# Convolution and soft mixture of experts on one core: the tap softmax in token layout, its result sent through a DRAM buffer into the diagonals of zeroed band tiles

## The chip, the cores and the metric

The kernel runs on one core of a Trainium2 chip. Such a core has a matrix engine (PE, with its weight loads shown apart as PEld), a vector engine (DVE), a scalar engine (ACT), a general engine (POOL), and an engine that only issues transfers (SP, its queue is SPq in the profile). Each engine works through its own list of instructions in order; they meet only at semaphores. Transfers between DRAM and on-chip memory (SBUF) run on 16 DMA engines. The metric is the device time of one execution in microseconds (us); lower is better.

## The reference, cut to what matters

Two layers in a row: a convolution over 7 tokens whose weights are a softmax made per token and head, and a soft mixture of experts over all 28672 tokens.

```python
# attention-like convolution: B, S, D = 8, 3584, 192; H, K = 8, 7 (24 channels a head)
w = exp(weight_gen - max(weight_gen, -1));  w = w / (sum(w, -1) + 1e-09)      # per token and head
x_pad = concatenate([zeros(B, 6, D), x], 1);  x_unf = x_pad[:, s + k]           # 7 rows a token
out = einsum('bshk,bskhg->bshg', w, x_unf)                                      # (B, S, 192)
# soft mixture: N = 28672 tokens, 8 experts with 4 slots each, F = 1024
logits = x @ phi                                                                # (N, 32)
d = softmax over tokens of logits;  slot_input = d.T @ x                        # (32, 192)
slot_out[e] = relu(slot_input[e] @ w1[e]) @ w2[e]
y = (softmax over slots of logits) @ slot_out
```

Everything is float32.

## The kernel before

**Tiling.** The 3584 tokens of a batch are cut into 35 groups of 104 tokens, a group into 4 blocks of 26 (`T`). So there are 280 groups. A block is convolved by one matmul per half of the heads: the stationary operand is a band matrix of 128 rows (4 heads with 32 input rows each) by 26 tokens, whose entry at row j + k, token j is the weight of tap k. The moving operand holds the input rows of the same 4 heads on the diagonal of a tile whose other parts are zero (`xbd`, in `big`), so that each head meets its own weights only. One call of `conv(p)` (L228) does a pair of groups, 16 matmuls, each recorded as two passes; there are 140 pairs, p = 0 to 139.

**Band tiles.** Seven groups make a superstep s (`SGG`, 40 of them). For each, `loadw` (L176) brings two copies of the taps: one in token rows, from which only the maximum is taken, and one already laid out by the host in band rows. `tap_top` (L181, DVE) takes the maximum of the 7 taps; `tap_spread` (L187, POOL) multiplies it by a mask; `tap_rows` (L194, PE) is a matmul with the constant `near`, which carries the maxima to the band rows (`pmx`); `tap_sub` (L199, DVE) and `tap_exp` (L203, ACT) follow; `band_make` (L206, POOL) multiplies the result by `mask2` into the full band tile. There are three band tiles and four taps tiles.

**Normalisation.** The softmax is not divided before the convolution. Each head has a 25th column of ones in `xbd` (`GX` = 25), so each matmul also gives the sum of the exponentials. `conv_sum` (L243, ACT) takes it out, `conv_inv` (L251, DVE) inverts it for two pairs at once, and `conv_out` (L255, DVE) multiplies it in while it copies the pair out of PSUM into `tm`.

**The rest of the main loop.** `xpose` (L264) turns the pair on PE and `xpose_out` copies it out; after each unit of 8 pairs (`UNITS`) come `logits` (L294), a running maximum, and `dispatch` (L356), which adds the unit to the slot inputs. Two pairs make a slot k of the loop at L523. After the main loop come the experts (L723 to L822) and the output phase (L834 to L846), which only multiplies, copies out and stores 22 MB.

**What sets the order.** All the engines' lists are written in one order: a planner (`op` and `model`, L480 to L693) is given for each step its engine, a cost, what it reads and writes, and for transfers a delay to landing; the order on PE and SP is the order in which the steps are listed, the other engines are chosen by due time. The opening (L376 to L436) is written out by hand. SP issues all transfers and is strictly in order, so a transfer that waits for a buffer holds up all those behind it. Transfers also share eight rotating semaphores, so a transfer cannot be issued before the one eight issues earlier has landed.

Of the kernel before, what the change touches and what calls it, by code (L numbers as in the profile page):

```python
# [8 lines left out]
F32 = mybir.dt.float32  # L9
# [7 lines left out]
GX = GW + 1  # L17
# [8 lines left out]
TAPS = NBC * KT  # L26
# [3 lines left out]
WARM = 9, 5  # L30
# [11 lines left out]
def conv_soft_moe(ctx, tc, xh, wh, phi, w1a, w1b, w2, out):  # L42
# [15 lines left out]
    NXH, HBC = 5, NBC // 2  # L58
    XB = 4 * HBC * GX
    big = keep.tile([128, NXH * XB], F32, name="big")  # L60
# [43 lines left out]
    NTM, NCV, NTAP, NBAND = 2, 3, 4, 3  # L104
    xbd = big.rearrange("p (i h c) -> p i h c", i=NXH, h=4)
    HB = NBC // 2


    taps = [fix.tile([128, 2, TAPS], F32, name=f"taps{i}") for i in range(NTAP)]
    bands = [fix.tile([128, T, NBC], F32, name=f"band{i}") for i in range(NBAND)]  # L110
# [5 lines left out]

    pmx = ps_l.tile([128, 512], F32, name="pmx")
    topP = pmx[:, 0:TAPS].rearrange("p (q l) -> p q l", q=KT)
# [13 lines left out]
    def warm(k):  # L132
        to = ps_t.tile([128, 4, 128], F32, tag="pt", name=f"warm{k}")[:, 0]
        for _ in range(WARM[k]):
# [3 lines left out]
    V.memset(one, 1.0)  # L138
    V.memset(xbd[:, 0:2, 0], 0.0)
    G.memset(xbd[:, 0:2, 1], 0.0)  # L140
    V.memset(xbd[:, 0:2, 2], 0.0)
    A.copy(xbd[:, 0:2, 3], zero.unsqueeze(1).to_broadcast([128, 2, HBC * GX]))
    ident = keep.tile([128, 128], F32, name="ident")
    make_identity(nc, ident)
    near = keep.tile([128, 128], F32, name="near")
    G.memset(near, 1.0)
    G.affine_select(out=near, in_=near, compare_op=ALU.is_ge, fill=0.0, base=0,
                    pattern=[[1, 128]], channel_multiplier=-1)
    G.affine_select(out=near, in_=near, compare_op=ALU.is_ge, fill=0.0, base=KT - 1,
                    pattern=[[-1, 128]], channel_multiplier=1)  # L150
    mask = keep.tile([128, 1, 32], F32, name="mask")
    maskT = keep.tile([128, 1, 32], F32, name="maskT")
    mask2 = keep.tile([128, 32, 1], F32, name="mask2")
    own = keep.tile([128, KT, 1], F32, name="own")

# [7 lines left out]
    eps = keep.tile([128, 1], F32, name="eps")  # L163
    V.memset(eps, EPS)
    for t in cvs:

        A.copy(t[:, 0 : 16 * GX], one.to_broadcast([128, 16 * GX]))

    def loadx(j):

        s, part = divmod(j, 2)
        z = slice(part * HBC * GX, (part + 1) * HBC * GX)
        for h in range(4):
            SY.dma_start(xbd[32 * h : 32 * h + 32, j % NXH, h], xh[s, h, :, z])  # L174

    def loadw(s):  # L176
        SY.dma_start(taps[s % NTAP], wh[s])

    tops = {}

    def tap_top(s):  # L181

        tops[s] = pa.tile([128, NBC, 1], F32, tag="top", name=f"top{s}")
        V.tensor_reduce(out=tops[s][:, :, 0], op=ALU.max, axis=AX.X,  # L184
                        in_=taps[s % NTAP][:, 0].rearrange("p (l k) -> p l k", k=KT))

    def tap_spread(s, eng=G):  # L187

        tops[s] = pa.tile([128, KT, NBC], F32, tag="spread", name=f"spread{s}"), tops[s]
        eng.tensor_tensor(out=tops[s][0], in0=own.to_broadcast([128, KT, NBC]),  # L190
                          in1=tops[s][1].rearrange("p l o -> p o l").to_broadcast([128, KT, NBC]),
                          op=ALU.mult)

    def tap_rows(s):  # L194

        P.matmul(pmx[:, 0:TAPS], near, tops[s][0].rearrange("p q l -> p (q l)"),  # L196
                 start=True, stop=True)

    def tap_sub(s):  # L199
        r = taps[s % NTAP][:, 1]  # L200
        V.tensor_tensor(out=r, in0=r, in1=pmx[:, 0:TAPS], op=ALU.subtract)  # L201

    def tap_exp(s):  # L203
        A.activation(taps[s % NTAP][:, 1], taps[s % NTAP][:, 1], AF.Exp)  # L204

    def band_make(s, lo=0, hi=HB, eng=G):  # L206

        l = slice(2 * lo, 2 * hi)
        r = taps[s % NTAP][:, 1].rearrange("p (q l) -> p q l", q=KT)[:, :, l]
        w = bands[s % NBAND]  # L210
        for j, n in ((0, 3 * KT), (3 * KT, T - 3 * KT)):
            k = min(n, KT)
            eng.tensor_tensor(out=w[:, j : j + n, l].rearrange("p (a k) l -> p a k l", k=k),  # L213
                              in0=r[:, 0:k].unsqueeze(1).to_broadcast([128, n // k, k, 2 * (hi - lo)]),
                              in1=mask2[:, j : j + n].rearrange("p (a k) o -> p a k o", k=k)
                              .to_broadcast([128, n // k, k, 2 * (hi - lo)]), op=ALU.mult)
# [11 lines left out]
    def conv(p):  # L228
        cv = cvs[p % NCV]
        for par in range(2):  # L230
            s, g = divmod(2 * p + par, SGG)
            for c in range(2):
                for blk in range(4):
                    bc = (4 * g + blk) * 2 + c
                    o = 4 * GX * (2 * par + (c ^ par))
                    j, b = divmod(s * NBC + bc, HBC)
                    P.matmul(cv[32 * blk : 32 * blk + T, o : o + 4 * GX],  # L237
                             bands[s % NBAND][:, :, bc],
                             xbd[:, j % NXH, :, b * GX : (b + 1) * GX], start=True, stop=True)

    wss = {}

    def conv_sum(p):  # L243

# [706 lines left out]
```

## Time and profile before

| | us |
|---|---|
| median of 3 runs | 344.33 |
| lowest and highest | 342.26, 345.93 |
| span of the profiled execution | 345.3 |
| DVE, ACT, POOL busy in it | 249.9, 161.7, 198.8 |
| first convolution matmul begins | 8.56 |
| first matmul of the output phase begins | 282.44 |

The page gives no other time of the profiled execution than its span, which lies 1.0 us above the median of the runs. Three stretches are told apart below: the opening until the loop runs evenly, the main loop until the last convolution, and what follows (experts and output). In the rows quoted, the first number of a piece in the chain of waits or of the timeline is its start in us, the second its length; in the groups of instructions it is busy us and mean ns of one, then the idle time of the engine ahead of them.

### The profile page before, as it was taken

Reading aid. Unit: us, or ns where it says so; the run is one execution under the profiler, and the core shown is the slowest. Engines: PE = TensorE matmul, PEld = TensorE weight load, DVE = VectorE, ACT = ScalarE, POOL = GpSimd, SP = SyncE. Lnnn points to the kernel's source line nnn. Section 1 sums busy time; section 2 is a strip of 40 time slices with the busy share of each in tenths; the row PEclk is TensorE's granted clock in tenths of the full one; section 3 lists DMA queues with packets and bytes.
Section 4 is the critical chain, followed back from the end, with each engine's and each line's share of the span. In section 5 each row is a group of like instructions: output and inputs, shape, how many; then the busy total and the mean of one; then the engine's idle time right before and its main releaser. Section 6 shows DMA issues by size and latency. Waiting matters only on the chain.

```text
span 345.3 us, 16352 instructions
## 1 busy us (share of the span) xinstructions
PE 306.8 (89%) x6896; PEld 222.2 (64%) x6896; DVE 249.9 (72%) x550; ACT 161.7 (47%) x428; POOL 198.8 (58%) x261
## 2 busy tenths in 40 slices
PE   8789999899999998999999999899997988799600
PEld 6567777687778876778778777678784952124100
DVE  7766877878788886897887868777864759965400
ACT  6535454455645654456445544454632237534300
POOL 8679648679489785868778568586601720000000
PEclk9999999999999999999999999999999999975555
DMA  6787788877877777677876867966589009999995
GB/s 197 215 260 196 214 223 196 246 205 221 215 217 228 211 235 189 199 207 205 241 210 176 237 173 204 260 172 180 154 307 364 6 2 398 395 403 399 395 404 204
DMA packets 33001, 80.82 MB, mean 234 GB/s; under 512 B 7072, under 2 KB 7456, under 8 KB 32928
## 3 DMA queue, kind: packets, MB, share of 16 engines
q1 hardware_dynamic: 32928, 79.77, 74.7%
q8 instruction: 55, 0.90, 1.2%
q14 instruction: 18, 0.15, 0.2%
HBM read 57.38 MB, written 22.36 MB: 231 GB/s over the span
## 4 chain that ended last, share of the span: by engine, by line
PE 58%; DMA 19%; DVE 9%; ACT 4%; issue 3%; SPq 2%; POOL 1%; DVEq 0%; ACTq 0%; POOLq 0%
PE cv L237 25%; PE pt L272 12%; DMA taps<-wh 8%; DMA out<-big 7%; PE pmx L196 6%; PE ls L301 6%; PE acb L365 5%; DMA big<-xh 4%; DVE big L841 3%; PE hpb L765 2%; PE so L786 2%; DVE cT L455 1%; DVE top L184 1%; SPq L174 1%; DVE tm L258 1%
## 5 line engine op out<-in xcount | busy, mean ns | idle before, releaser
L213 POOL TENSOR_TENSOR band<-taps,mask 128x588 f32<-128x588 f32 (+3 forms) x158 | 121.3, 798 | 31.9 <-ACT taps L204 23.1
L237 PE MATMUL cv<-big,band 128*26 128x100 f32 x4480 | 120.4, 252 | 6.2 <-POOL band L213 1.5
L237 PEld LDWEIGHTS cv<-big,band 128*26 128x26 f32 x4480 | 101.0, 128 | 36.4 <-issue 29.0
L258 DVE TENSOR_TENSOR tm<-cv,ws 128x384 f32<-128x384 f32 x140 | 72.9, 551 | 6.7 <-DVE ws L253 1.0
L277 ACT COPY cm<-pt 128x312 f32<-128x312 f32 x140 | 51.9, 423 | 44.5 <-PE pt L272 44.0
L247 ACT ACTIVATE ws<-cv,eps 128x16 f32<-128x16 f32 x140 | 37.7, 272 | 58.0 <-PE cv L237 46.2
L272 PE MATMUL pt<-ident,tm 122*128 122x122 f32 x420 | 59.2, 277 | 0.7 <-ACT cm L277 0.7
L272 PEld LDWEIGHTS pt<-ident,tm 122*128 122x128 f32 x420 | 43.4, 141 | 16.4 <-issue 9.9
L253 DVE RECIPROCAL ws<-ws 128x32 f32<-128x32 f32 x70 | 24.3, 348 | 29.9 <-ACT ws L247 29.4
L190 POOL TENSOR_TENSOR spread<-own,top 128x392 f32<-128x392 f32 x37 | 31.2, 843 | 24.3 <-DVE top L184 13.0
L834 PE MATMUL po<-cT,so 32*128 32x468 f32 (+3 forms) x256 | 38.1, 726 | 5.2 <-DVE big L841 4.5
L841 ACT COPY big<-po 128x936 f32<-128x936 f32 (+2 forms) x25 | 22.4, 902 | 27.1 <-PE po L834 15.2
L196 PE MATMUL pmx<-spread,near 128*128 128x392 f32 x80 | 33.7, 503 | 1.6 <-POOL spread L190 0.8
L841 DVE COPY big<-po 128x884 f32<-128x884 f32 (+2 forms) x24 | 25.4, 1071 | 12.8 <-DMA out<-big 10.5
L834 PEld LDWEIGHTS po<-cT,so 32*128 32x128 f32 (+1 forms) x256 | 12.4, 188 | 29.7 <-DVE big L841 23.1
L184 DVE TENSOR_REDUCE top<-taps 128x56 f32<-128x392 f32 x40 | 22.1, 551 | 12.3 <-DMA taps<-wh 11.2
L301 PE MATMUL ls<-cm,phi_sb 128*32 128x208 f32 (+1 forms) x576 | 29.5, 334 | 0.3 <-issue 0.3
L204 ACT ACTIVATE taps<-taps 128x392 f32<-128x392 f32 x40 | 21.0, 525 | 17.5 <-DVE taps L201 14.5
L365 PE MATMUL acb<-tm,dt 128*32 128x193 f32 x536 | 26.6, 328 | 0.7 <-DVE dt L346 0.4
L301 PEld LDWEIGHTS ls<-cm,phi_sb 128*32 128x32 f32 x576 | 19.9, 109 | 4.6 <-issue 0.6
L201 DVE TENSOR_TENSOR taps<-taps,pmx 128x392 f32<-128x392 f32 x40 | 22.1, 553 | 0.4 <-PE pmx L196 0.4
L92 POOL TENSOR_TENSOR LT<-LT,sm 128x576 f32<-128x576 f32 (+1 forms) x16 | 18.1, 1132 | 5.1 <-DVE sm L90 4.9
(113 smaller groups left out, 256.0 us busy)
## 6 DMA issues: line engine op xcount, KB each, us to landing
big<-xh SPq DMA_DIRECT2D x320, 87.5 KB, 3.9
taps<-wh SPq DMA_DIRECT2D x40, 392.0 KB, 4.6
out<-big SPq DMA_DIRECT2D x23, 468.0 KB, 6.5
out<-big SPq DMA_DIRECT2D x24, 442.0 KB, 6.4
big<-w SPq DMA_DIRECT2D x8, 768.0 KB, 6.9
w1a_sb<-w1a SPq DMA_DIRECT2D x16, 256.0 KB, 3.9
w1b_sb<-w1b SPq DMA_DIRECT2D x8, 256.0 KB, 3.7
out<-big SPq DMA_DIRECT2D x2, 234.0 KB, 2.4
```

Of the source, the lines that this page charges most:

```text
L190: eng.tensor_tensor(out=tops[s][0], in0=own.to_broadcast([128, KT, NBC]), in1=tops[s][1].rearrange("p l o -> p o l").to_broadcast([128, KT ...
L196: P.matmul(pmx[:, 0:TAPS], near, tops[s][0].rearrange("p q l -> p (q l)"), start=True, stop=True)
L213: eng.tensor_tensor(out=w[:, j : j + n, l].rearrange("p (a k) l -> p a k l", k=k), in0=r[:, 0:k].unsqueeze(1).to_broadcast([128, n // k, k ...
L237: P.matmul(cv[32 * blk : 32 * blk + T, o : o + 4 * GX], bands[s % NBAND][:, :, bc], xbd[:, j % NXH, :, b * GX : (b + 1) * GX], start=True, ...
L247: A.activation(wss[p // 2][:, p % 2], cvs[p % NCV][:, 0 : 16 * GX].rearrange("p (h w) -> p h w", w=GX)[:, :, GW:], AF.Identity, bias=eps[: ...
L258: V.tensor_tensor(out=tms[u % NTM][:, pr, 1 : 2 * D + 1].rearrange("p (h w) -> p h w", w=GW), in0=cv[:, :, 0:GW], in1=wss[p // 2][:, p % 2 ...
L272: P.transpose(pt[:, i, 0:TR], tm[0:TR, pr, 1 + 128 * i : 129 + 128 * i], ident[0:TR, 0:TR])
L277: copy(cms[u][:, pr].rearrange("p i b j -> p (i b) j"), pts.pop(p).rearrange("p i (b j) -> p (i b) j", j=32)[:, :, 0:T])
L301: P.matmul(lp[32 * blk : 32 * blk + 32, 0:n, par, 0:T], phi_sb[:, 2 * par + i, :], cm[:, 0:n, 1 if i else 2 * par, blk, :], start=(i == 0) ...
L365: P.matmul(ac[32 * q : 32 * q + 32], dt[:, g, :], tm[:, g // 2, o : o + D + 1], start=(g < 4), stop=(g + 4 >= 2 * n))
L834: P.matmul(po[dst : dst + hi - lo, at, 0 : n * T], so[32 * q : 32 * q + 32, lo:hi], cT[32 * q : 32 * q + 32, g0 : g0 + n, 0:T], start=True ...
L841: (V.tensor_copy if done[1] % 2 else A.copy)(ot.rearrange("p (q c) -> p q c", c=n * T), po[:, 0 : len(qs), 0 : n * T])
```

## The change

The softmax of the taps is finished before the convolution, in the layout the taps come in: 104 partitions (26 tokens by 4 heads), 7 taps, 112 columns. The superstep of the taps becomes 14 groups (`PG`, 20 of them, 7 pairs each); that of the input rows stays at 7 groups (40 loads, now in three buffers of a whole superstep instead of five of a half). Maximum, difference, exponential, sum, reciprocal and product are plain operations on that tile (`seven`, `tap_sub`, `tap_exp`, `tap_sum`, `tap_inv`, `tap_mul`). The maximum matmul, `near`, both masks, `tap_spread` and `band_make` go away, and so do the ones column (24 columns a head instead of 25), `conv_sum` and `conv_inv`; `conv_out` is a plain copy, three of four on ACT.

The finished weights reach the band tile through DRAM. `turn_out` writes them into a buffer `turned` whose rows have 14 places for the taps, of which 7 stay zero (`clear` zeroes them once); `turn_in` reads the same buffer with a row length of 13 places, which shifts each token by one row and so puts the taps on the diagonal of the band, zeros included. Places outside the four diagonal blocks of a band tile are zeroed once at the start. Both buffers, the taps tiles and the band tiles are double.

```diff
-GX = GW + 1
+PG = 14
+NPS = B * NG // PG
+PL = PG * 4 * 2
+ZK = 14
-WARM = 9, 5
+WARM = 9, 14
-    NTM, NCV, NTAP, NBAND = 2, 3, 4, 3
+    NTM, NCV, NTAP = 2, 4, 2
+    taps = [fix.tile([PT, KT, PL], F32, name=f"taps{i}") for i in range(NTAP)]
+    bands = [fix.tile([128, T, PL], F32, name=f"band{i}") for i in range(2)]
+    turned = [dram.tile([T, ZK, 4, PL], F32, name=f"turned{i}") for i in range(2)]
...
+            SY.dma_start(xbd[h:128:4, t % NXS, h], xh[t, h])
...
+        m = pa.tile([PT, 4, PL], F32, tag="seven", name=f"{tag}{s}_{l.start}", bufs=1)[:, :, 0:n]
+        V.tensor_tensor(out=m[:, 0:3], in0=t[:, 0:3], in1=t[:, 3:6], op=op)
+        V.tensor_tensor(out=m[:, 0], in0=m[:, 0], in1=m[:, 1], op=op)
+        V.tensor_tensor(out=m[:, 0], in0=m[:, 0], in1=m[:, 2], op=op)
+        last(m[:, 3], m[:, 0], t[:, 6])
...
+    def turn_out(s, l, by=(SY, SY, SY, SY)):
+        for h in range(4):
+            by[h].dma_start(turned[s % 2][:, 0:KT, h, l], taps[s % NTAP][h:PT:4, :, l])
+    BANDS = ((0, 8), (2, 16), (10, 24), (18, T))
+    def turn_in(s, l, by=(SY, SY, SY, SY)):
+        rows = turned[s % 2].rearrange("j k h l -> (j k h) l")
+        w = 4 * (ZK - 1)
+        for a, (lo, hi) in enumerate(BANDS):
+            at = w * lo + 32 * a
+            by[a].dma_start(bands[s % 2][32 * a : 32 * a + 32, lo:hi, l],
+                            rows[at : at + w * (hi - lo)]
+                            .rearrange("(j w) l -> w j l", w=w)[0:32, :, l])
...
+    def conv_out(p, copy=A.copy):
+        copy(tms[u % NTM][:, pr, 1 : 2 * D + 1], cvs[p % NCV][:, 0 : 2 * D])
...
+    loadw(0, 0, 32)
+    loadx(0)
+    loadw(0, 32, PL)
+    clear(0)
+    tap_top(0, FIRST)
...
+    turn_out(0, FIRST, both)
...
+    turn_in(0, FIRST, both)
+    turn_out(0, REST, both)
...
+    turn_in(0, REST, both)
...
+    loadw(1)
+    loadx(1)
+    clear(1)
+    conv(0)
...
+    turn_at = {s: max(2, (PG // 2 * (s - 1) - 1) // 2) for s in range(1, NPS)}
...
+            if k == max(1, kr - 3):
+                for f, e, c in tap_costs:
+                    op(e, c, [], [("w", s % NTAP)] + ["seven"] * (f != tap_exp), f, s, ALL, due=3.0)
+            if k == max(1, kr - 1):
+                op(SP, 1.8, [("w", s % NTAP)], [("turned", s % 2)], turn_out, s, ALL, late=2.5)
+            if k == kr:
+                op(SP, 1.8, [("turned", s % 2)], [("band", s % 2)], turn_in, s, ALL, late=3.0)
```

In the opening, `FIRST` is the columns of the first 4 groups of superstep 0, `REST` those of the other 10, and `both` lets SP and ACT issue two transfers each. `XB`, the expert weights' places in `big` and the number of output buffers (17 instead of 14) follow from the new size of `xbd`.

Three places in the order of the engines matter below. The first is PE in the middle of the loop. Before, where `cv` is the PSUM tile of a pair, `pt` that of a transpose and `pmx` the maxima:

```order
L301 MATMUL ls<-cm_1175,phi_sb 32x8x26 x16
L272 MATMUL pt_1479<-ident,tm_91 128x122 x3
L272 MATMUL pt_1483<-ident,tm_91 128x122 x3
L196 MATMUL pmx<-spread_1366,near 128x392
L237 MATMUL cv_94<-big,band_89 26x100 x16
L324 MATMUL acb<-mq,sel_132 32x5 x4
L237 MATMUL cv_95<-big,band_89 26x100 x16
```

And the same place of the changed kernel, after the same kind of unit:

```order
L297 MATMUL ls<-cm_1122,phi_sb 32x8x26 x16
L268 MATMUL pt_1402<-ident,tm_92 128x122 x3
L268 MATMUL pt_1406<-ident,tm_92 128x122 x3
L250 MATMUL cv_95<-big,band_87 26x96 x16
L320 MATMUL acb<-mq,sel_130 32x5 x4
L250 MATMUL cv_96<-big,band_87 26x96 x16
```

The matmul into `pmx` is gone, the others stand as they stood, with 96 columns instead of 100. The second place is SP in the middle of the loop; before, a superstep of 7 groups is one load of taps and eight of input rows:

```order
L177 DMA taps_86<-wh 128x784
L174 DMA big<-xh 32x700 x8
L702 DMA w1a_sb<-w1a 128x512
L177 DMA taps_87<-wh 128x784
L174 DMA big<-xh 32x700 x8
```

In the changed kernel a superstep of 14 groups is this, where `turned` is the DRAM buffer:

```order
L217 DMA turned_90<-taps_84 26x7x112 x4
L164 DMA big<-xh 32x1344 x4
L227 DMA band_86<-turned_90 32x8x112
L227 DMA band_86<-turned_90 32x14x112 x2
L227 DMA band_86<-turned_90 32x8x112
L167 DMA taps_84<-wh 104x784
L164 DMA big<-xh 32x1344 x4
L666 DMA w1a_sb<-w1a 128x512
```

Eight transfers of the round trip have come in, and as many loads of input rows have gone. The third place is the opening of the changed kernel; on SP, up to the input rows of the third superstep of 7 groups:

```order
L167 DMA taps_84<-wh 104x7x80
L211 DMA turned_90<-band_87 26x1568 x2
L217 DMA turned_90<-taps_84 26x7x32 x2
L227 DMA band_86<-turned_90 32x8x32
L227 DMA band_86<-turned_90 32x14x32
L217 DMA turned_90<-taps_84 26x7x80 x2
L227 DMA band_86<-turned_90 32x8x80
L227 DMA band_86<-turned_90 32x14x80
L167 DMA taps_85<-wh 104x784
L164 DMA big<-xh 32x1344 x4
L211 DMA turned_91<-band_87 26x1568 x2
L164 DMA big<-xh 32x1344 x4
```

The taps of the second superstep (`taps_85`) are asked for only behind the whole round trip of the first, where before the taps of two supersteps were the first two transfers. On ACT, at the same place, the rows behind the two copies of the constants are:

```order
L273 COPY cm_318<-pt_319 128x312
L273 COPY cm_318<-pt_327 128x312
L256 COPY tm_92<-cv_95 128x384
L193 ACTIVATE taps_85<-taps_85 104x784
L273 COPY cm_318<-pt_373 128x312
```

The exponential of the second superstep stands behind the copy of pair 4 (`cv_95`, the second use of that tile).

More of the change, by code (lines that the diff above doesn't have):

```diff
@@ L137, in conv_soft_moe @@
     warm(0)
[L138 to L142, printed above, removed]
+    eps = keep.tile([128, 1], F32, name="eps")
+    V.memset(xbd[:, 0, 0], 0.0)
+    G.memset(xbd[:, 0, 1], 0.0)
+    A.copy(xbd[:, 0, 2], zero.to_broadcast([128, NBC * GW]))
+    V.memset(xbd[:, 0, 3, 0 : NBC * GW // 2], 0.0)
+    G.memset(xbd[:, 0, 3, NBC * GW // 2 :], 0.0)
+    V.memset(bands[0][:, 0 : T // 2], 0.0)
+    A.copy(bands[1][:, 0:ZK], zero.unsqueeze(1).to_broadcast([128, ZK, PL]))
+    G.memset(bands[0][:, T // 2 :], 0.0)
+    V.memset(eps, EPS)
     ident = keep.tile([128, 128], F32, name="ident")
     make_identity(nc, ident)
[L145 to L154, printed above, removed]
     sel4 = keep.tile([128, 4, NS], F32, name="sel4")
@@ L162, in conv_soft_moe, with loadx @@
     mq = keep.tile([128, 5], F32, name="mq")
[L163 to L164 removed]
     for t in cvs:
[L167 to L172, printed above, removed]
+        A.copy(t, zero.to_broadcast([128, 512]))
+    def loadx(t):
         for h in range(4):
[L174 to L177 removed]
@@ L179, in conv_soft_moe @@
[L179 to L216, printed above, removed]
+            SY.dma_start(xbd[h:128:4, t % NXS, h], xh[t, h])
```

257 lines of the change are left out of this document (105 added, 152 removed).

## The prediction

> **What bounds the kernel now.** I read the page first, then the chain of waits in the loop, then the timeline of its two ends, then the DMA views.
>
> ```profile
> PE 306.8 (89%) x6896; PEld 222.2 (64%) x6896; DVE 249.9 (72%) x550; ACT 161.7 (47%) x428; POOL 198.8 (58%) x261
> PE 58%; DMA 19%; DVE 9%; ACT 4%; issue 3%; SPq 2%; POOL 1%; DVEq 0%; ACTq 0%; POOLq 0%
> L196 PE MATMUL pmx<-spread,near 128*128 128x392 f32 x80 | 33.7, 503 | 1.6 <-POOL spread L190 0.8
> 82.31 1.55 PE cv L237 x64
> 83.85 0.78 PE pt L272 x6
> 84.63 0.67 PE pmx L196 x2
> ...
> 107.79 1.31 PE acb L365 x24
> ```
>
> PE is busiest and holds most of the chain. Inside the loop the chain is PE almost without a break: two pairs convolved in 1.55 us, two transposes in 0.78, and, 40 times in the run, 0.67 for the maxima. The ends of the loop, in PE's timeline:
>
> ```profile
> 8.56 0.92 PE L237 MATMUL cv<-big,band 128*26 128x100 f32 x32
> ...
> 21.77 0.92 PE L237 MATMUL cv<-big,band 128*26 128x100 f32 x32 [1.47 <-POOL band L213]
> ...
> 257.45 0.89 PE L237 MATMUL cv<-big,band 128*26 128x100 f32 x32
> ```
>
> Pair 0 starts at 8.6, pair 7 at 21.8, and pair 139 ends at 258.3. So I split the span: 21.8 up to pair 7, 236.5 for the 133 pairs from there (1.778 a pair), and 87.0 behind the last one; together 345.3. Pair 7 is the cut because it is the first pair that needs the second band tile of the changed kernel.
>
> **The maxima leave PE.** Four of the 40 matmuls into `pmx` stand ahead of pair 7. The other 36 by 0.67 are 24.1 us, 0.181 a pair, all of it on the chain; their removal leaves 1.597. The convolutions, transposes, logits and dispatches alone come to about 1.51 (four times 1.55 + 0.78, then 1.41 and 1.31, for 8 pairs). The difference of 0.09 is waits and drains; I leave them in, because the new loop has waits of its own. The logits' piece, from the chain, and that of the running maximum, from the timeline:
>
> ```profile
> 100.94 1.41 PE ls L301 x30
> 104.46 0.21 PE L324 MATMUL acb<-mq,sel 128*32 128x5 f32 x8
> ```
>
> **Narrower matmuls.** Columns fall from 100 to 96. If time followed columns, 4% of 1.55 in each of 70 slots would save 4.3 us. It does not follow them: 64 passes in 1.55 are 24 ns each, while the logits need 44 ns for 208 columns (32 passes in 1.41) and the dispatch 41 ns for 193, which is 21 ns for 100; and passes of only 5 columns still take 26 ns. I take nothing. The Trainium skill speaks here too: TensorE: Matmul & The Clock Gate, the section "Wait — 56ns, not 53.3ns?", says that matmuls never start closer than about 25 ns, however few the columns. By that rule the gain is 0, by proportion it would be 4.3; the 24 ns and 26 ns of this trace agree with the rule.
>
> **The other engines.** DVE loses L258 and L253, and L184 and L201 with 22.1 each, 141 in all. It gains, per superstep, twice four small operations (336 and three times 112 elements; at the 1.43 ns an element of L258 and at least 0.2 each, 1.1 together) and a reciprocal of about 1.0, so 20 x 3.2 = 64, and 35 copies of 0.5: 250 becomes about 190. POOL loses 121.3 + 31.2 and gains 40 products of 784 elements, about 1.5 each by the two forms of L213: 199 becomes about 107. ACT loses 37.7 and 21.0, gains 105 copies of about 0.5 and 20 exponentials of 0.9: 162 becomes about 173. None comes near PE, so their terms are zero, and what hides them is PE's 1.6 a pair.
>
> ```profile
> L258 DVE TENSOR_TENSOR tm<-cv,ws 128x384 f32<-128x384 f32 x140 | 72.9, 551 | 6.7 <-DVE ws L253 1.0
> L253 DVE RECIPROCAL ws<-ws 128x32 f32<-128x32 f32 x70 | 24.3, 348 | 29.9 <-ACT ws L247 29.4
> L247 ACT ACTIVATE ws<-cv,eps 128x16 f32<-128x16 f32 x140 | 37.7, 272 | 58.0 <-PE cv L237 46.2
> L213 POOL TENSOR_TENSOR band<-taps,mask 128x588 f32<-128x588 f32 x77 | 91.0, 1182 | 31.6 <-ACT taps L204 22.8 <-issue 8.1
> L213 POOL TENSOR_TENSOR band<-taps,mask 128x140 f32<-128x140 f32 x77 | 32.6, 423 | 0.0
> L184 DVE TENSOR_REDUCE top<-taps 128x56 f32<-128x392 f32 x40 | 22.1, 551 | 12.3 <-DMA taps<-wh 11.2
> L201 DVE TENSOR_TENSOR taps<-taps,pmx 128x392 f32<-128x392 f32 x40 | 22.1, 553 | 0.4 <-PE pmx L196 0.4
> L190 POOL TENSOR_TENSOR spread<-own,top 128x392 f32<-128x392 f32 x37 | 31.2, 843 | 24.3 <-DVE top L184 13.0
> L204 ACT ACTIVATE taps<-taps 128x392 f32<-128x392 f32 x40 | 21.0, 525 | 17.5 <-DVE taps L201 14.5
> ```
>
> **The queue of SP.** Per 14 groups SP issued 16 loads of rows, 2 of taps and about 1 of weights; now 8, 1, 1, and 8 for the round trip. At the median 0.42 of an x issue that is 7.6 us of a superstep of 7 x 1.597 = 11.2. In the order, `turn_in(s)` can go once the band of s - 2 is read, one whole superstep before its own first pair. Ahead of it stand four x loads; with four issues, a weight and 4.6 to land it is there after 8.4, so 2.8 us are spare. Behind a `turn_in` that waits for `turn_out` to land stand the taps of s + 2 and the next x load, each with half a superstep in hand. I cost these waits at zero; the cover is that lead, and without it PE would stand still for what is missing, 20 times.
>
> ```profile
> L174 SPq DMA_DIRECT2D big<-xh x320: 310/416/2205, 2.5 to 245.2; - x160
> DMA to landing us min/median/max: 2.0/3.9/6.5
> DMA to landing us min/median/max: 2.9/4.6/6.8
> phi_sb<-phi SPq DMA_DIRECT2D x1, 64.0 KB, 2.4
> ```
>
> (The second row is the x loads', the third the taps'.)
>
> **The DMA engines.** A superstep now moves 1.38 MB of rows, 0.33 of taps and 0.31 of weights in large packets, then 0.33 out and 0.63 in through 728 + 1408 = 2136 packets of 448 bytes, 134 per DMA engine. What such a packet costs, no row says.
>
> ```profile
> 60.00:100.00 40.00, 38.70 (x1003) 30.33 (x1006) 33.26 (x80) 20.81 (x63) 29.93 (x37) 1.00 0.79 219
> 285.00:300.00 15.00, 11.48 (x120) 3.27 (x116) 15.00 (x18) 9.92 (x11) 0.00 (x0) 1.00 1.02 399
> q1 hardware_dynamic: 32928, 79.77, 74.7%
> ```
>
> (The last two columns of a window are the DMA engines' busy share and GB/s.) At full share the loop moves 219 / 0.79 = 277 GB/s, the output 391. Large packets: 2.02 MB, 5.2 to 7.3 us; I take 7.3, the loop's own. Small ones: from below by bytes at 391, 18 ns each; from above the mean packet of this run, 74.7% of 16 x 345.3 over 32928, 125 ns. Nearest are the 512-byte packets of `phi`: 8 per engine landed 0.4 us later than the quickest x load with its 2, so at most about 50 to 80 ns, and that beside other traffic. I take 26 ns, the loop's rate by bytes, because x packets with their own overhead run at that rate. Then 3.5 us, 10.8 in all: just under 11.2, so hidden, with 4% to spare. That is the weakest term.
>
> **The opening.** This is where the change costs. Before, both first taps were on the way at 0.8 and DVE began at 4.1.
>
> ```profile
> 0.80 1.28 ACT L142 ACT_TABLE_LOAD   x1 [0.80 <-PEq L940]
> ...
> 4.11 0.55 DVE L184 TENSOR_REDUCE top<-taps 128x56 f32<-128x392 f32 x1
> L142 ACT COPY big<-zero 128x1400 f32<-128x1400 f32 x1 | 1.4, 1358 | 0.0
> L167 ACT COPY cv<-one 128x400 f32<-128x400 f32 x3 | 1.3, 487 | 0.0
> 0.00:10.00 10.00, 8.22 (x68) 6.75 (x72) 8.00 (x19) 6.40 (x9) 8.66 (x21) 1.00 0.71 222
> 10.00:20.00 10.00, 8.54 (x204) 6.34 (x208) 6.66 (x18) 6.07 (x18) 7.29 (x19) 1.00 0.78 214
> ```
>
> Now ACT first fills about 1344 + 1568 + 4 x 512 elements (2.8 + 2.3 from 2.1 on), so the first exponential ends near 7.5; sum, reciprocal and product take it to 9.2. Out (two issues each on SP and ACT, 0.8, and 2.4 to land) and in (the same) put pair 0 at about 15. The other columns start on DVE behind the first reciprocal, at 8.6: maximum 1.1, difference 1.1, exponential 0.7, sum 1.1, reciprocal 0.8, product 1.1 give 14.7 with the hops, written by 17.9, read by 21.2. ACT's half of that reading holds up the copy of pair 0 behind it, for which nobody waits before pair 3 is done. Only then does SP ask for the second taps (landed 21.6) and the rows of groups 7 to 13 (23.4). The exponential of superstep 1 stands on ACT behind the copy of pair 4, which needs pair 3 and so those rows: 26.6. Its sum, reciprocal and product end at 31, four issues and a landing at 35.1, a taps load, four issues and a landing at 39.6. Pair 7 starts at 40, against 21.8. If all six landings took 2.0 it is 37; at the loop's medians of 3.9 and 4.6, 47 to 50. I take 2.4, the one landing of a small load in the opening: about 4.1 MB move up to 25 us, where before 4.4 moved up to 20 (the two windows above). The 14 warming matmuls sit in idle PE time and cost nothing.
>
> **The tail** stays: 87.0. The output is stored at DMA share 1.02, so three more buffers there bring nothing.
>
> **The sum:** 40 + 133 x 1.597 = 252.4, and 87.0: 339.4 against 345.3, that is 5.9 less. The median of the runs lies 1.0 under the span: 338.4.
>
> **The rivals.**
> *The small packets make DMA the bound (slower).* At price t a superstep takes 7.3 + 0.134 t us. It binds above 29 ns; even with before at 258.3 - 40 = 218.3 for 133 pairs, 11.5 a superstep, 31 ns; slower by 1% from 33 ns. At 36 ns: 12.1, so 40 + 230 + 87 = 357, by the runs 356. For it: DMA is already at 0.79. Against: half as many x packets, and more landing slack. The Trainium skill, DMA: Bandwidth & Descriptors, section Specifications, says that full rate needs 512 bytes and that below it a DMA engine reads, modifies and writes; no run here shows a packet of 448, so I give this a fourth of the chance and no more.
> *Convolution passes get longer.* Their weights now lie 448 bytes apart instead of 224. If the 3 ns above the 21 by columns are weight loads, and they double: 32 x 3 x 133 = 12.8 us: 352, by the runs 351. No row speaks for it but that gap; the logits' contiguous weights show none.
> *The opening eats it all.* Landings at the loop's medians, pair 7 at 47: 346, by the runs 345. For it: in the loop they are that long. Against: in the opening fewer bytes move.
> *The opening is shorter, and before's leftover waits go with the saturated DVE.* Pair 7 at 37 and 1.55 a pair, between the 1.51 of bare matmuls and 1.597: 330, by the runs 329.
> *The change takes nothing off PE* cannot be: the order shows no `pmx` row left.
>
> **How the numbers follow.** Forecast 0.40 (331 to 341), shorter opening 0.08, opening eats it 0.15, small packets 0.25, longer passes 0.12. A measurement of this kernel can tell about 1% from no change, 3.4 us. Faster: the forecast and the shorter opening, 0.48. Same: the late opening and half of the longer passes, 0.21. Slower: the packets and the other half, 0.31. The range from 328 to 356 leaves out the dearer half of the packets' cases and little below.
>
> **What would show it.** Pair 7 at 40 (the first pass that reads the second band tile); 1.6 a pair from there; 24 ns a pass; no `pmx`; DMA share near 0.95 in the loop at about 265 GB/s; `turn_in` landing before its first pair; 87 behind the last pair. A PE that waits for `band<-turned` at each seventh pair, with DMA share at 1, makes me wrong by the packets; one that waits only in the first 50 us, by the opening.

## The result: slower by a quarter, and the profile after

The changed kernel takes 432.51 us in the median of 4 runs (429.8 to 433.82), the kernel before 344.8 beside it (342.26 to 345.93). The ratio is 1.254, with a 95% interval of 1.244 to 1.264. The profiled execution has a span of 431.8 us against 345.3: 86.5 us more. The predicted time was 338.4, the range 328 to 356.

First the page of the changed kernel: the engines' busy time, the DMA queue of SP, and the chain that ended last.

```profile
PE 299.4 (69%) x6834; PEld 225.6 (52%) x6834; DVE 207.9 (48%) x477; ACT 170.1 (39%) x372; POOL 125.0 (29%) x104
q1 hardware_dynamic: 68389, 88.40, 69.4%
PE 30%; DMA 25%; SPq 17%; DVE 11%; ACT 4%; issue 4%; POOL 4%; ACTq 0%; DVEq 0%; POOLq 0%
```

PE held 58% of the chain before and holds 30% now. SP's queue had 2% and has 17%; DMA and DVE have grown too. No engine is busy all the time, and the DMA queue is at 69%: nothing is saturated over the whole span, so the time must be in things that wait for each other.

PE's timeline gives the three stretches with the cuts of the prediction, pair 0, pair 7 and the last pair:

```profile
16.39 2.78 PE L250 MATMUL cv<-big,band 128*26 128x96 f32 x64 [7.78 <-DMA band<-turned]
...
51.91 1.50 PE L250 MATMUL cv<-big,band 128*26 128x96 f32 x32 [16.65 <-DMA band<-turned]
...
156.75 1.55 PE L250 MATMUL cv<-big,band 128*26 128x96 f32 x64
...
344.25 0.86 PE L250 MATMUL cv<-big,band 128*26 128x96 f32 x32
```

| | before | predicted | after |
|---|---|---|---|
| up to pair 7 | 21.8 | 40 | 51.9 |
| 133 pairs from there | 236.5 | 212.4 | 293.2 |
| one pair of them | 1.778 | 1.597 | 2.205 |
| behind the last pair | 87.0 | 87.0 | 86.7 |

The opening lost 30 us against before, the loop 57, the tail nothing. The third row of the fence is a convolution of two pairs that runs without a wait: 1.55 us. The loop's window of the changed kernel (busy us and count of PE, PEld, DVE, ACT, POOL, then granted clock, DMA share, GB/s) and the longest waits between pair 7 and the end of the last pair, of DVE and PE and then of SP:

```profile
60.00:250.00 190.00, 143.13 (x3625) 114.25 (x3617) 96.43 (x247) 81.39 (x195) 66.30 (x43) 0.87 0.76 201
```

```profile
DVE top L174 <- DMA taps<-wh: 76.2, 16, 10.5
...
PE acb L320 <- DVE mq L306: 24.9, 9, 6.9
PE acb L361 <- DVE dt L342: 23.2, 4, 6.7
PE cv L250 <- DMA band<-turned: 16.6, 1, 16.6
```

```profile
SPq L164 <- PE cv L250: 36.3, 15, 6.1
SPq L217 <- POOL taps L205: 8.8, 1, 8.8
```

PE is busy 143 of 190 us, where the kernel before had 185. From pair 7 to the end of the last pair it stands still for 64.7 of 293.2 us, where the kernel before stood for 5.8 of 236.6. Its matmuls are busy for 228.5 us there, hardly less than the 230.8 before, although the maxima have left: the granted clock is 0.87 instead of 1.00, so they run slower too, and the last section comes back to this. In the loop PE does not wait for the band tiles: the one wait of 16.6 us is the one ahead of pair 7 itself. For 48.1 us it waits for DVE, and DVE waited 76.2 us, 16 times, for the *taps* of the softmax. One such place, from the timeline of all engines:

```profile
156.60 0.37 SPq L167 DMA_DIRECT2D taps<-wh  x1
...
162.66 0.51 DVE L174 TENSOR_TENSOR top<-taps 104x336 f32<-104x336 f32 x1 [6.84 <-DMA taps<-wh]
...
164.01 0.70 DVE L342 STREAM_TRANSPOSE dt<-dd 128x512 f32<-128x512 f32 x1
...
164.77 2.80 PE L361 MATMUL acb<-tm,dt 128*32 128x193 f32 x32 [6.47 <-DVE dt L342]
```

SP asks for the taps at 156.6. DVE, which works through its list in order, has stood at their maximum since 155.8 and goes on at 162.7. Behind it in DVE's list stands the transposition of `dd` that the dispatch needs, so PE stands still for 6.5 us for something that has nothing to do with the taps. The circle closes over SP: with PE the convolutions are late, the loads of input rows wait for their buffer (`SPq L164 <- PE cv`), and behind them in SP's list stands the next load of taps.

SP itself has little room to catch up. Its issues (min/median/max ns of one):

```profile
L217 SPq DMA_DIRECT2D turned<-taps x80: 784/823/1475, 9.3 to 320.4; - x80
```

```profile
L164 SPq DMA_DIRECT2D big<-xh x160: 469/587/1658, 2.3 to 330.5; - x160
```

```profile
L227 SPq DMA_DIRECT2D band<-turned x80: 313/477/2103, 13.4 to 328.1; - x80
```

At these medians, eight x loads, four issues each way, a load of taps (0.37) and a weight (0.59, from the timeline) are 4.70 + 3.29 + 1.91 + 0.96 = 10.9 us of a superstep, where the prediction had 7.6. With the means in the place of the medians (0.64, 0.86, 0.54) it is near 12. A superstep takes 7 x 2.205 = 15.4.

The opening, in the chain of the changed kernel:

```profile
17.04 4.46 DMA turned<-taps
...
22.48 5.15 DMA taps<-wh
...
33.49 0.87 ACT taps L193
...
38.72 0.87 SPq L217
...
41.37 2.31 DMA turned<-taps
...
45.59 6.12 DMA band<-turned
```

### The profile page after: what moved, and what is told of

Same layout as the page of the kernel before. It is cut to its first block, busy times and chain, and to the rows that moved or that the text cites. A ratio compares the mean times of both kernels' runs of the same rounds, so it can differ in the third digit from the quotient of the medians.

```text
span 431.8 us, 15659 instructions
## 1 busy us (share of the span) xinstructions
PE 299.4 (69%) x6834; PEld 225.6 (52%) x6834; DVE 207.9 (48%) x477; ACT 170.1 (39%) x372; POOL 125.0 (29%) x104
## 4 chain that ended last, share of the span: by engine, by line
PE 30%; DMA 25%; SPq 17%; DVE 11%; ACT 4%; issue 4%; POOL 4%; ACTq 0%; DVEq 0%; POOLq 0%
DMA taps<-wh 15%; PE cv L250 11%; PE pt L268 7%; SPq L164 6%; SPq L227 4%; PE acb L361 4%; DMA turned<-taps 4%; SPq L217 3%; POOL taps L188 3%; DMA band<-turned 3%; PE ls L297 2%; DMA out<-big 2%; DVE big L802 2%; PE po L795 2%; SPq L804 2%
## 5 line engine op out<-in xcount | busy, mean ns | idle before, releaser
L250 PE MATMUL cv<-big,band 128*26 128x96 f32 x4480 | 126.5, 269 | 43.0 <-DMA band<-turned 31.5
L273 ACT COPY cm<-pt 128x312 f32<-128x312 f32 x140 | 53.6, 425 | 52.8 <-PE pt L268 52.6
L188 POOL TENSOR_TENSOR taps<-taps,top 104x784 f32<-104x784 f32 (+2 forms) x21 | 37.3, 1774 | 121.0 <-DVE top L184 79.2
L256 ACT COPY tm<-cv 128x384 f32<-128x384 f32 x104 | 49.8, 481 | 46.0 <-PE cv L250 32.5
L205 POOL TENSOR_TENSOR taps<-taps,sum 104x784 f32<-104x784 f32 (+2 forms) x21 | 37.5, 1784 | 69.7 <-DVE sum L201 52.3
L174 DVE TENSOR_TENSOR top<-taps 104x336 f32<-104x336 f32 (+2 forms) x21 | 10.3, 492 | 95.0 <-DMA taps<-wh 93.4
L193 ACT ACTIVATE taps<-taps 104x784 f32<-104x784 f32 (+2 forms) x21 | 17.4, 827 | 91.9 <-POOL taps L188 91.8
L361 PE MATMUL acb<-tm,dt 128*32 128x193 f32 x536 | 33.5, 398 | 23.5 <-DVE dt L342 23.2
L361 PEld LDWEIGHTS acb<-tm,dt 128*32 128x32 f32 x536 | 19.3, 133 | 31.9 <-DVE dt L342 24.0
L256 DVE COPY tm<-cv 128x384 f32<-128x384 f32 x36 | 19.8, 549 | 16.2 <-PE cv L250 16.1
L174 DVE TENSOR_TENSOR sum<-taps 104x336 f32<-104x336 f32 (+2 forms) x21 | 10.9, 519 | 23.2 <-ACT taps L193 23.2
L83 POOL TENSOR_TENSOR LT<-LT,rm 128x576 f32<-128x576 f32 (+1 forms) x16 | 18.1, 1132 | 12.6 <-DVE rm L81 12.3
```

The source lines that it names most:

```text
L174: V.tensor_tensor(out=m[:, 0:3], in0=t[:, 0:3], in1=t[:, 3:6], op=op)
L188: G.tensor_tensor(out=t, in0=t, in1=tops.pop(s).to_broadcast([PT, KT, l.stop - l.start]), op=ALU.subtract)
L205: G.tensor_tensor(out=t, in0=t, in1=tsums.pop(s).to_broadcast([PT, KT, l.stop - l.start]), op=ALU.mult)
L250: P.matmul(cv[32 * blk : 32 * blk + T, o : o + 4 * GW], bands[s % 2][:, :, i], xbd[:, t % NXS, :, b * GW : (b + 1) * GW], start=True, stop ...
L256: copy(tms[u % NTM][:, pr, 1 : 2 * D + 1], cvs[p % NCV][:, 0 : 2 * D])
L273: copy(cms[u][:, pr].rearrange("p i b j -> p (i b) j"), pts.pop(p).rearrange("p i (b j) -> p (i b) j", j=32)[:, :, 0:T])
```

## The experiments

Two theories at first. A: the load of the taps comes late and holds up DVE, so PE, so SP, so the next taps. B: SP's own issue time sets the pace of the loop. A third came up on the way, C: the round trip's traffic on the DMA engines, whether by its packets of 448 bytes or by its bytes. Each kernel below was run once with a profile, beside a run of the kernel before that gave 341 to 346 us; differences of some 5 us between two of them are not read. In the table at the end of this section the loop is always the time from pair 7 to the end of the last pair in that kernel's own trace. DVE's waits for taps are given for whole executions, opening included; in the changed kernel they come to 93.4 us.

**The planner is told that taps land late** (theory A alone, nothing else moved on SP):

```diff
-                op(SP, 0.4, [], [("w", s % NTAP)], loadw, s, late=2.5)
+                op(SP, 0.4, [], [("w", s % NTAP)], loadw, s, late=7.0)
```

> Only the planner's guess of when a load of taps has landed goes from 2.5 to 7.0 us, so tap_top moves behind other work in the lists of DVE, POOL and ACT; SP's list stays row for row. Theory A (a late load of taps holds up DVE, so PE, so the x loads on SP, so the next taps): DVE's waits for taps fall from 93 us to under 40, a superstep from 15.4 to about 13, the run to 370 to 395. Theory B (SP's own issue time, 11.0 us a superstep, and its waits set the pace): 415 to 435, as before.

It took 410.46 us; the loop fell from 293.2 to 270.5, and DVE's wait for taps from 93.4 to 48.3. A part of the loss hung on the place of the maximum in DVE's list, but not the forecast amount: the time lies between the ranges of the two theories.

**Taps asked for earlier, into a third tile:**

```diff
-    NTM, NCV, NTAP = 2, 4, 2
+    NTM, NCV, NTAP = 2, 4, 3
-            if s >= NTAP and k == max(1, kr - 6):
+            if s >= 2 and k == max(1, kr - 9):
```

> A third taps buffer (in a part of w1b that is loaded last), and each load of taps is listed three slots earlier on SP; the number of transfers is the same. Theory A: DVE's waits for taps under 10 us, the run at 355 to 385. Theory B: SP has as much to issue, 415 to 435.

411.81 us, loop 270.0. DVE still waited 42.3 us for taps in the old tiles and 25.4 in the new one. The gain is real and small; neither theory had forecast it.

**No softmax after superstep 0:**

```diff
-            if k == max(1, kr - 3):
+            if k == max(1, kr - 3) and s < 0:
```

> Leaves out the tap softmax of supersteps 1 to 19 (maximum, difference, exponential, sum, reciprocal, product), so raw taps go through the round trip; all transfers stay. Theory A: nothing on DVE waits for taps any more, the run at 350 to 380. Theory B: SP's list is unchanged, 410 to 430. If the DMA engines themselves are the bound, also 410 to 430, with a DMA share near 1.

388.67 us, loop 255.4, again between the two theories. Nobody waits for taps on DVE any more, and SP hardly waits for anybody; the largest waits of SP in the loop of this kernel are these:

```profile
SPq L164 <- PE cv L250: 6.6, 7, 2.2
SPq L164 <- PE pt L268: 5.7, 11, 1.1
SPq L448 <- PE cv L250: 4.8, 2, 3.0
```

SP issues most of the time instead: in the records of this trace its 328 issues of the loop come to 221 us, and with some 0.045 between two they fill about 235 of the loop's 255. SPq has 25% of the chain. Here B comes near to being the floor.

**The writes of the round trip issued by POOL:**

```diff
-                op(SP, 1.8, [("w", s % NTAP)], [("turned", s % 2)], turn_out, s, ALL, late=2.5)
+                op(PO, 4.0, [("w", s % NTAP)], [("turned", s % 2)], turn_out, s, ALL, (G, G, G, G), late=2.5)
```

> The 76 turn_out transfers of the loop are issued by POOL behind its own product, not by SP: 3.3 us of 11.0 of SP's issue time a superstep and its waits for the product go. Theory B: a superstep falls by 3 to 4 us, the run to 365 to 385. Theory A: taps are asked for some 3 us earlier of the 6 they are late, the run at 385 to 410.

395.42 us, loop 257.4. SP is relieved of 66 us of issues, POOL takes 49 for the same 76 (0.64 each), and DVE still waits 52.9 us for taps. The time lies in the range given for A, but both A and B are at work: each edit leaves the other limit standing. The loop is 36 us shorter; not all of it need be issue time, since SP no longer stands for POOL's product either (8.8 us in the loop above). The Trainium skill, DMA: Bandwidth & Descriptors, section "Issuing engines are not separate DMA queues", says that issuing from several engines saves only the sequencer's time, which is usually small beside the transfer. Here an issue of 0.82 us stood beside landings of 2.3 and 4.5 us in the chain of the opening, and 76 of them moved away were worth those 36 us: in this kernel that time was not small.

**All three edits together:**

> Three edits at once: a third taps tile with its load listed nine slots ahead, the planner's landing time for taps raised from 2.5 to 7.0 us, and the 76 turn_outs of the loop issued by POOL. Theory of both (late taps on DVE, and SP's issue time, hold up the loop together, each filling in when the other is taken away): the loop falls to near PE's own work, 212 to 228 us for 133 pairs, so 52 + 212..228 + 87, 350 to 367. If only the taps' wait mattered, the run stays at 395 to 410, as the single edits did; if a third limit stands behind (DMA engines with small packets), 370 to 390, with the DMA share of the loop near 1.

371.73 us, loop 232.1: 61 us less than the changed kernel, yet 5 over the upper end of what the theory of both allowed, and inside the range given for a third limit, though the DMA share of the loop is 0.87 and not near 1. DVE's wait for taps has gone down to 8.8 us, and PE's waits for DVE in the loop from 48.1 to 6.3.

**No softmax, and the writes issued by POOL:**

> Leaves out the softmax of supersteps 1 to 19, all transfers stay; and the 76 turn_outs of the loop are issued by POOL instead of SP. Theory of SP's issue time as floor of the run without softmax (loop 255 us, of them 232 of issue): 65 us of issue leave SP, so the loop falls to PE or DMA, 212 to 225; with 45 before and 87 behind, 344 to 357. Theory that the small packets on the DMA engines are that floor: loop stays at 245 to 258, run 377 to 392.

367.58 us, loop 236.4: 19 less than with SP issuing, but not the 212 to 225 of theory B. A third limit stands there. The loop's window:

```profile
60.00:250.00 190.00, 165.10 (x4598) 133.74 (x4592) 71.44 (x164) 91.81 (x233) 65.13 (x83) 0.98 0.90 240
```

The DMA engines are now busy for 0.90, where the changed kernel had 0.76. Beside the run above this says a second thing: with the taps asked for early and planned late, the loop with softmax (232.1) is no longer than this one without (236.4). So the arithmetic of the softmax can be hidden; what cost was its wait. The comparison is not clean, though. POOL works in order too, and in this run the writes at the head of its list wait for transfers, which holds ACT and through it DVE:

```profile
POOL turned L217 <- DMA big<-xh: 56.9, 8, 11.6
DVE sm L89 <- ACT LT L86: 33.0, 10, 10.2
ACT LT L86 <- POOL LT L83: 32.6, 12, 6.6
```

PE's waits for ACT and DVE in this loop come to 10.5 us, so a part of its 236.4 comes with the move to POOL and not from the DMA engines.

**No softmax and no round trip** (beside the edit of "No softmax"):

```diff
-            if k == max(1, kr - 1):
+            if k == max(1, kr - 1) and s < 2:
-            if k == kr:
+            if k == kr and s < 2:
```

> Leaves out the softmax of supersteps 1 to 19 and the round trip through DRAM of supersteps 2 to 19; the loads of taps, of input rows and of weights stay. It shows what PE, ACT and DVE make of the loop by themselves. If the limit that stands behind the taps' wait and SP's issue time (loop at 232 to 236 us in the two runs before) is the DMA engines' load with the round trip, the loop falls to 205 to 220 (1.54 to 1.65 a pair); if it is PE with its partners, it stays at 230 to 237.

333.66 us, loop 199.6, that is 1.50 a pair: lower than any theory had put it. The loop's window shows PE without gaps:

```profile
60.00:250.00 190.00, 188.54 (x5544) 155.43 (x5536) 85.35 (x198) 108.64 (x279) 30.13 (x29) 1.00 0.69 211
```

**Softmax without round trip,** the fourth corner:

> The softmax stays for all supersteps; left out is the round trip through DRAM of supersteps 2 to 19, its issues on SP and its bytes, so that all later pairs read the first two band tiles. It fills the fourth place beside the changed kernel (loop 293 us), the run without softmax (255) and the run without both (200). If the late taps hold DVE and with it PE only because SP's issues and the transfers of the round trip delay the taps' loads: loop 200 to 215, run 334 to 350. If the softmax holds up DVE's list by itself, by its place in the planner's order: loop 235 to 260, run 370 to 395.

378.8 us, loop 238.3. DVE waits for taps, and SP for convolutions, though the DMA engines are at 0.56 and SP has ten issues a superstep left:

```profile
DVE top L174 <- DMA taps<-wh: 45.5, 14, 9.5
```

```profile
SPq L164 <- PE cv L250: 89.3, 28, 7.8
```

So the circle of theory A needs neither the traffic of the round trip nor its issues, and the expectation that the softmax holds up DVE's list by its place came true. The four corners, loop in us:

| | without round trip | with round trip |
|---|---|---|
| without softmax | 199.6 | 255.4 |
| with softmax | 238.3 | 293.2 |

The softmax costs 38.7, the round trip 55.8, both 93.6: they add up.

**Long packets for the round trip** (same bytes, same number of transfers):

```diff
+            if s > 0:
+                flat = turned[s % 2].rearrange("j k h l -> (j k h) l")[h * T * KT : (h + 1) * T * KT]
+                by[h].dma_start(flat.rearrange("(j k) l -> j k l", k=KT), taps[s % NTAP][h:PT:4])
...
+                by[a].dma_start(bands[s % 2][32 * a : 32 * a + 32, lo:hi],
+                                rows[0 : 32 * (hi - lo)].rearrange("(w j) l -> w j l", w=32))
```

> From superstep 1 on the round trip's transfers carry the same bytes in the same number of transfers on the same queue, but run over contiguous rows of the buffer (3136 and 3584 to 6272 bytes a packet instead of 448), so that the weights land in the wrong places. If packets under 512 bytes were what makes the changed kernel slow: 340 to 370. If they cost by their bytes, as the 25 ns a packet of its trace say, and the loop is set by SP's issues and the late taps: 420 to 435; somewhat less, 395 to 420, if the issue time of these transfers on SP falls with the number of packets.

424.19 us, loop 285.8: 7 less. And with the three edits of the loop:

> The three edits of the loop (third taps tile, landing time 7.0, turn_out issued by POOL), and the round trip in long packets as in the run above. If the small packets are the limit that is left there (loop 232 us): loop 205 to 220, run 344 to 360. If bytes count and not packets: 228 to 236, run 367 to 375.

365.07 us, loop 226.6, against 232.1 with short packets: 5.5 less, just below the range given for bytes. Both differences are little more than the 5 us that single runs leave open. In the changed kernel's records the 40584 packets of 448 bytes have a median of 25 ns and a mean of 31. Of the rule that the prediction weighed (the Trainium skill, DMA: Bandwidth & Descriptors, section Specifications: full rate from 512 bytes) that leaves a loss of at most some 2% of the run, not the cause.

**Input rows into neighbouring partitions** (made on the run without softmax):

```diff
-            SY.dma_start(xbd[h:128:4, t % NXS, h], xh[t, h])
+            SY.dma_start(xbd[32 * h : 32 * h + 32, t % NXS, h], xh[t, h])
```

> Leaves out the softmax of supersteps 1 to 19, and loads the input rows into 32 neighbouring partitions instead of every fourth one, so that they land in the wrong places; packets and bytes stay. If it is the partition step that makes an x issue 0.59 us instead of the 0.42 of the kernel before, the issue falls to about 0.42, SP's 232 us by 25, and with SP as the floor the run falls from 388.7 to 362 to 370. If it is the longer rows (1344 elements instead of 700), the issue and the run stay, 385 to 391.

The issue does fall, to the 0.42 of the kernel before:

```profile
L164 SPq DMA_DIRECT2D big<-xh x160: 310/419/1785, 2.3 to 298.4; - x160
```

So it is the step of four partitions that made an x issue 0.17 us dearer, not its longer rows. The load of a weight, whose form is the same in all runs and which mostly stands right behind x loads, moves with it: its median issue is 0.42 in the kernel before and in this run, and 0.59 in the changed kernel. So the time recorded for an issue depends on the transfer issued ahead of it too. But the run came out at 404.07, longer by 15 than without this edit: the DMA share of the loop rose from 0.83 to 0.97, and the median x packet (5376 bytes) from 221 to 369 ns in the records. Why such packets are slower here is not settled; the kernel before sent its 2800-byte packets to neighbouring partitions too, at a median of 126 ns.

**The opening** (the taps of superstep 1 asked for behind those of superstep 0, their softmax ahead of the second reading):

```diff
     loadw(0, 32, PL)
+    loadw(1)
...
+    tap_top(1, ALL)
+    tap_sub(1, ALL)
+    tap_exp(1, ALL)
     turn_in(0, REST, both)
-    loadw(1)
```

> The changed kernel with another opening only: the taps of superstep 1 are asked for right behind those of superstep 0, and their softmax is listed ahead of the second half of superstep 0's round trip. If pair 7 is late because of the order of the opening: pair 7 at 40 to 46 instead of 51.9 and the run 6 to 12 us shorter, 421 to 427. If the loop's pace was set by SP and the taps anyway, a shorter opening may be lost again in the loop: 430 to 435.

Pair 7 came at 47.0 instead of 51.9, but the run took 431.2: the loop grew to 296.6, so the gain was lost there, as the second expectation had it.

**All edits together:**

> All three edits of the loop and the edit of the opening. Theory of both: pair 7 at 40 to 46, 212 to 228 for the loop, 87 behind: 339 to 361. If a third limit holds the loop at 250: 377 to 383.

370.41 us, pair 7 at 46.9, loop 236.0, between the two ranges given. Of the versions that compute the whole this is the lowest, though the 371.73 of the three edits cannot be told from it, and it is 29 us above the 341.07 of the kernel before beside it. None of the runs points to a version that beats the kernel before: even in it, opening and loop come to 283, where the kernel before has 258.

| kernel | time | pair 7 at | loop |
|---|---|---|---|
| changed kernel (median of 4; its trace) | 432.5 | 51.9 | 293.2 |
| taps planned late | 410.5 | 51.6 | 270.5 |
| third taps tile, earlier load | 411.8 | 52.8 | 270.0 |
| writes issued by POOL | 395.4 | 50.5 | 257.4 |
| these three | 371.7 | 51.5 | 232.1 |
| these three, long packets | 365.1 | 50.7 | 226.6 |
| long packets alone | 424.2 | 51.0 | 285.8 |
| other opening alone | 431.2 | 47.0 | 296.6 |
| these three, other opening | 370.4 | 46.9 | 236.0 |
| no softmax | 388.7 | 45.2 | 255.4 |
| no softmax, writes by POOL | 367.6 | 43.6 | 236.4 |
| no softmax, x to neighbouring partitions | 404.1 | 47.6 | 268.3 |
| no round trip | 378.8 | 52.2 | 238.3 |
| neither softmax nor round trip | 333.7 | 46.5 | 199.6 |

## Why the prediction was wrong

It forecast the wrong side, by 94 us. Point by point:

- **The maxima leave PE: right.** Without softmax and round trip a pair takes 1.50, and the loop 36.9 us less than before (236.5 to 199.6). 24.1 of that are the maxima, some 4 the narrower passes of the next point; the rest, some 9, lay in the 0.09 a pair of "waits and drains" that the prediction left in.
- **Narrower matmuls at nothing: wrong, by a small term.** In the same view, PE's timeline, 64 passes without a wait take 1.61 us before and 1.55 with 96 columns (first row before, second the run with neither softmax nor round trip):

```profile
85.23 1.61 PE L237 MATMUL cv<-big,band 128*26 128x100 f32 x64
63.91 1.55 PE L250 MATMUL cv<-big,band 128*26 128x96 f32 x64
```

That is 4%, as by columns, and 0.06 in each of 66 slots is 4 us of the loop. The 1.55 of before was read from the chain, where a piece ends with the start of the next; there the run with neither has 1.48. Its 64 starts lie within 1.30 us, on average 21 ns apart, so a floor of 25 ns does not show in this kernel. The 41 ns of a dispatch came from a chain row with 24 of its 32 passes; in the timeline all 32 take 1.51 us, 47 ns each, which is 24 ns for 100 columns and no gap.

- **The other engines off the path: near in busy time, wrong in what follows from it.** DVE, POOL and ACT came to 207.9, 125.0 and 170.1 against 190, 107 and 173. But "what hides them is PE's 1.6 a pair" counted work and not order. DVE was half idle and still held up PE, because its list is in order and the operation at its head waited for a load.
- **The waits on SP at zero: the step that failed.** The prediction said that behind a `turn_in` "stand the taps of s + 2 and the next x load, each with half a superstep in hand". The loop lists the load of the taps only three slots (six pairs, 9.6 us at the forecast pace) ahead of their maximum. Of these the landing alone took 4.4 to 6.8 us where it stands in the loop's chain, and the rest was spent in SP's queue, behind x loads that wait for convolutions. The lead existed for the band, and the loop's PE indeed never waits for the band; it did not exist for the taps. This is the 38.7 of the softmax. With the taps asked for early and planned late, and the writes on POOL, PE's waits for DVE fall to 6.3 us. The other 55.8 of the loop is the round trip's, in the next two points.
- **SP's issues at 0.42 each, 7.6 us: mis-sized.** The median was 0.82 for a write of the round trip, 0.48 for a reading, 0.59 for an x load: 10.9 a superstep, 12 with the means. Against a superstep of 10.5 us on PE (7 x 1.50) that alone leaves no room, and little against the 11.2 of the forecast. Moving the writes to POOL was worth 36 us with softmax and 19 without.
- **The DMA engines at 10.8, "just under 11.2, so hidden": well sized, wrongly judged.** Without round trip the share of 0.69 in a superstep of 10.5 is 7.2 us, against 7.3. With it, in the run where DMA is busiest for its cause (no softmax, writes by POOL), 0.90 of 12.4 is 11.2. That is more than PE's 10.5, so it cannot hide there. But engines that never idle would still do a superstep in 11.2 us, the pace of the forecast, which makes 13 of the 36.8 us that lie between that run and the one without round trip. For the rest, longer landings, the four readings' issues and POOL's list may all have a part; PE's matmuls alone are busy for 209.2 us there instead of 198.4. No run parts these, and this stays open.
- **Small packets (the rival at 0.25): the right side for the wrong reason.** They cost 5 to 7 us, and the median packet took 25 ns, beside the 26 of the forecast.
- **Longer passes: fell.** The passes became shorter.
- **The opening at 40: mis-sized; the rival "opening eats it all" had the cause, and with pair 7 at 47 was still 5 us short.** The writing of the ten later groups took 4.46 us from its last issue to its landing and the second taps 5.15, where 2.4 was taken for each, so the exponential of superstep 1 came at 33.5 and not at 26.6, and its weights were ready at 38.7 and not at 31. From there writing and reading took 13.0 us (38.7 to 51.7) and not 8.6: issues of 0.85 in place of 0.42, and a last landing of 6.12. That makes 7.7 + 4.4, the 11.9 us that pair 7 is late but for 0.2.
- **The tail at 87.0: right,** 86.7.

The signs that were to show the prediction wrong were also too narrow: it named a PE that waits for `band<-turned`. The loop has no such wait. The one that came, PE behind DVE behind a load, was not on the list: the softmax was costed by its busy time only.

## What to carry to other kernels

When a step with a load at its head is put on an engine that works in order, ask what stands behind it on that engine and how many slots ahead the load is issued on *its* queue; a half idle engine can still set the pace. Cost each issue of a transfer by its own shape and by the queue it stands in, and compare the sum with the superstep that the change is meant to reach, not with the one it starts from. To see what a chain of late things costs, take each cause out alone and then all together: here the single edits to the taps, the softmax and the writes gave 23 to 38 us each, and only the four corners showed what adds up to the whole.

## What the hardware showed that was not expected

- The time SP needs to issue a transfer depends on its form: 0.37 us for a flat tile of 104 partitions (taps), 0.42 for 32 neighbouring partitions, 0.59 for the same rows into every fourth partition, 0.82 for the 26 x 7 pieces of the writing, though the reading with 32 x 8 or 32 x 14 pieces takes 0.48. POOL issued the same writing in 0.64. It depends on the transfer ahead as well: the same weight load takes 0.42 or 0.59, as the x loads ahead of it do.
- A wait of PE costs more than itself. The same 6834 matmuls keep PE busy for 299.4 us in the changed kernel and for 270.7 in the run with neither softmax nor round trip; the dispatch behind the wait of 6.47 us took 2.80 for 32 passes, 88 ns each against 47 before. The granted clock of that stretch (the third number from the end) is 0.50:

```profile
164.77:167.57 2.80, 2.80 (x33) 1.44 (x34) 2.38 (x4) 0.86 (x1) 2.41 (x2) 0.50 0.76 214
```

Over the loop's window it is 0.87 where it was 1.00. Of the 93.6 us by which the changed loop is longer than that of the run with neither, 63.5 are PE standing still and 30.0 are its matmuls taking longer. The Trainium skill, TensorE: Matmul & The Clock Gate, section "Part 1: The HAM clock gate (the "warmup" mystery)", says that the clock is halved after an idle window of about 3.4 us; the 0.50 behind this wait agrees.
